# Layer 2's results turned to token rows by VectorE's 32x32 transposes instead of TensorE transposes, on one Trainium2 core

## The chip, the core and the metric

The kernel runs on one core of a Trainium2 chip. The metric is the device time of one execution in microseconds (us). TensorE (PE) multiplies, VectorE (DVE) and ScalarE (ACT) do the elementwise work, GpSimd (POOL) does almost nothing here, and SyncE (SP) issues every transfer, in program order.

## What is computed

```python
# q, k, v: (8 batches, 8 heads, 576 tokens, 64); x below is (4608 tokens, 512)
kv = einsum('bhsd,bhse->bhde', k, v)
out = einsum('bhsd,bhde->bhse', q, kv)                 # then rms-normalised per head
...
xn = x / rms * rms_g                                   # layer 1
x = (silu(xn @ w_gate) * (xn @ w_val)) @ w_out         # d_ff 1536
h = maximum(x @ w_in, 0.0)                             # layer 2
return h * h @ w_out2                                  # d_ff 2048, result (4608, 512)
```

## The kernel before

Activations are kept transposed: a block `j` holds 512 tokens as 4 tiles `c` of 128 features by 512 tokens. There are nine blocks. Every float32 product is done as three TensorE passes over a high and a low part of each operand (`split` makes the parts: ScalarE copies the high part at line 616, VectorE subtracts at line 617).

The work runs in stages of two blocks. Each stage has an x-stage (`x_stage`, the product with the first weight, line 711) and an h-stage (`h_stage`, the product with the second). Stages of layer 2 with two blocks use a seven-product scheme (Strassen-like), so their h-stage is `run_seven` (line 989): 28 steps of 12 matmuls, seven products `i` in the order 1, 2, 5, 6, 7, 3, 4, four steps each but for the first two, whose last steps come together. The stages of layer 2 are the blocks (0,1), (2,3), (4,5), (6,7) and, alone, (8). The lone block runs `run_last`, where activations are the stationary operand, so its result comes out as token rows by itself.

In an h-stage each step needs one operand tile `ho`, made from `raw` by `split`; the pool `hop` has three such tiles, so ScalarE starts tile k when TensorE has ended step k-3. For products 1, 2, 5 and 6 VectorE also updates `raw` with a subtraction (line 620). `h_result` takes a finished result: for product 2 (tiles 0 and 1 of the first block), product 7 (tiles 2 and 3 of the second) and product 3 (tiles 0 and 1 of the second) VectorE adds a saved copy (line 726); for product 4 (tiles 2 and 3 of the first block) ScalarE copies the PSUM bank (line 1042).

In layer 2 the result then lies as `c_t[j, c]`, features by tokens, and the output wants token rows. So during the next stage's x-stage `side_step` runs two kinds of step in turn, one every second tick (a tick comes after every six matmuls there): `out_tile` puts four TensorE transposes of 128x128 into a PSUM bank (line 1050), and `out_put` copies the bank with ScalarE (line 1058) and stores 128 rows of 2 KB (line 1061). That is four groups for a block, eight for a stage.

```python
    def tick():
        now[0] += 1
...
        for p, acc, step in (("side", "s", side_step), ("prep", "p", prep_step)):
```

Weights come as tiles `wt` of 512 KB, one for every 12 matmuls, in a ring of five (`W_RING`): the load of a tile is issued when TensorE has let go of the tile five before it. All loads and stores stand in SP's one queue. `after(n, fn)` issues something n ticks later. The last block's `out_halves` copies each finished PSUM bank in two halves, one on ScalarE, one on VectorE, and stores them.

Of the kernel before, what the change touches and what calls it, by code (L numbers as in the profile page):

```python
# [11 lines left out]
F32 = mybir.dt.float32  # L12
# [3 lines left out]
AF = mybir.ActivationFunctionType  # L16
# [27 lines left out]
def attn_moe_moe(  # L44
# [13 lines left out]
    nc = tc.nc  # L58
    B, S, DM = kv.shape[0], kv.shape[1], kv.shape[2] // 2
# [3 lines left out]
    KC = DM // 128  # L63
    T = 512
    NB = NT // T
    NQ = T // 128
# [10 lines left out]
    ps_att = ctx.enter_context(tc.tile_pool(name="ps_att", bufs=1, space=bass.MemoryType.PSUM))  # L77
# [8 lines left out]
    ident = const.tile([128, 128], F32, name="ident")  # L86
# [4 lines left out]
    x2d = [dram.tile([128, KC, T], F32, name=f"x2d{j}") for j in range(NB)]  # L91
# [4 lines left out]
    def new_tmp(name="t"):  # L96
        return tmp.tile([128, T], F32, tag="t", name=name)
# [182 lines left out]
    prep_q = deque()  # L280

    def prep_step(due=True):
        if prep_q and all(getattr(fn, "ready", lambda: True)() for fn in prep_q[0]):
            if not due and not all(getattr(fn, "landed", lambda: True)() for fn in prep_q[0]):
                return False
            for fn in prep_q.popleft():
                fn()
            return True
        return False
# [60 lines left out]
    def w_fetch():  # L350
        nxt = None if not streams[0] or len(w_have) == W_RING else next(w_todo, None)
        if nxt:
            pair, h, i = nxt
            while not all((key, h) in prepped for key in pair):
                assert prep_step(), nxt
            if isinstance(i, slice):
                wide.rotate(-1)
                t = xop.tile([128, 2, 2, 2, 256], F32R, tag=wide[0], name="ww")
                nc.sync.dma_start(out=t.bitcast(F32), in_=wd[pair][h][:, i])
                w_have.append((nxt, t))  # L360
                return
            t = wpool.tile([128, 2, 2, 256], F32R, tag="w", name="wt")
            nc.sync.dma_start(out=t.bitcast(F32), in_=wd[pair][h][:, i])
            w_have.append((nxt, [t[:, e] for e in range(2)]))
# [286 lines left out]
    def x_load(layer, blocks, b, q, rb):  # L651

        j, kh = blocks[int(b[1]) - 1], int(b[0]) - 1
        while layer == 1 and (j, 2 * kh + 1) not in x1_done:
            assert chain or due, j
            tick()
        t = raw_tile(q, rb, "xr")
        nc.sync.dma_start(out=t, in_=(x1d if layer == 1 else x2d)[j][:, 2 * kh:2 * kh + 2, :])
        return t
# [1 line left out]

    now = [0]
    due = {}
    side = deque()
    pace = {"side": 0.0, "prep": 0.0, "s": 0.0, "p": 0.0}

    def after(n, fn):
        due.setdefault(now[0] + n, []).append(fn)
# [4 lines left out]
        seq_n[0] += 1  # L673
        insort(chain, (t, seq_n[0], fn))

    def side_step():
        if side:
            for fn in side.popleft():
                fn()

    def tick():
        now[0] += 1
        for fn in due.pop(now[0], ()):
            fn()
        while chain and chain[0][0] <= now[0]:
            chain.pop(0)[2]()
        for p, acc, step in (("side", "s", side_step), ("prep", "p", prep_step)):
            pace[acc] += pace[p]
            while pace[acc] >= 1:
                if step is prep_step and prep_q and not prep_step(False):  # L690
                    pace[acc] = min(pace[acc], 2)
                    break
                pace[acc] -= 1
                if step is side_step:
                    step()

    def flush():
        while due:
            tick()
# [25 lines left out]
    def add(o, ps, t):  # L725
        nc.vector.tensor_tensor(out=o, in0=ps, in1=t, op=ALU.add)  # L726
# [8 lines left out]
    def x_stage(layer, blocks, early):  # L735
# [7 lines left out]
        for n, t in visits:  # L743
# [10 lines left out]
            if first[0] and (n, t) == (0, 2):  # L754
                while chain:
                    tick()
                t0 = now[0] + 1
                for j in range(stages[1][1][0], NB):
                    gap, period = (6, 47) if j < 5 else (8, 60)
                    if j == 2:  # L760
                        kv_events(j, t0, gap)
                        t0 += 28
                    o_events(j, t0, 5, t0 + (30 if j == 2 else 33), 4)
                    if j + 1 < B:
                        kv_events(j + 1, t0 + 17, gap)
                    t0 += period
# [69 lines left out]
                    tick()  # L836
            banks.extend([bk[2], bk[3], bk[0], bk[1]])

    c_t, late = {}, deque()

    def h_stage(layer, blocks, nxt):

# [188 lines left out]

    def h_result(layer, j, c, ps, t=None):

        if layer == 1:
            o = new_tmp("o")
        else:
            o = l2c.tile([128, T], F32, tag=f"c{c}_{j % 2}", name="c")
            c_t[j, c] = o
        if t is not None:
            add(o, ps, t)  # L1040
        else:
            nc.scalar.activation(out=o, in_=ps, func=AF.Copy)
        if layer == 1:
            after(5, lambda: nc.sync.dma_start(out=x2d[j][:, c, :], in_=o))

    def out_tile(j, i, pool=ps_att, tag=None):

        ps = pool.tile([128, DM], F32, tag=tag or "AB"[i % 2], name="ot")
        for c in range(KC):
            nc.tensor.transpose(  # L1050
                out=ps[:, c * 128:(c + 1) * 128], in_=c_t[j, c][:, i * 128:(i + 1) * 128], identity=ident
            )
        return ps

    def out_put(j, i, ps, eng, lag=2):
        t = new_tmp("ob")
        if eng is nc.scalar:
            nc.scalar.activation(out=t, in_=ps, func=AF.Copy)
        else:
            nc.vector.tensor_copy(out=t, in_=ps)  # L1060
        after(lag, lambda: nc.sync.dma_start(out=out[j * T + i * 128:j * T + (i + 1) * 128, :], in_=t))

    def out_halves(j, i, ps):
        rows = slice(j * T + i * 128, j * T + (i + 1) * 128)
        for eng, c in ((nc.scalar, slice(0, T // 2)), (nc.vector, slice(T // 2, T))):
            t = tmp.tile([128, T // 2], F32, tag="t", name="ob")
            if eng is nc.scalar:
                eng.activation(out=t, in_=ps[:, c], func=AF.Copy)
            else:
                eng.tensor_copy(out=t, in_=ps[:, c])  # L1070
            nc.sync.dma_start(out=out[rows, c], in_=t)

    def out_steps(blocks):
        st, got = [], {}
        for j in blocks:
            for i in range(NQ):
                st.append([lambda j=j, i=i: got.__setitem__((j, i), out_tile(j, i))])
                st.append([lambda j=j, i=i: out_put(j, i, got.pop((j, i)), nc.scalar)])
        return st


    with tc.manual_schedule():
        hops = [(hop, "hop")]
# [91 lines left out]
        for n, (layer, blocks) in enumerate(stages):  # L1175
            nxt = stages[n + 1] if n + 1 < len(stages) else None
            if layer == 2 and stages[n - 1][0] == 1:
                assert not chain
                l1.close()
                l2raw = l2.enter_context(tc.tile_pool(name="raw3", bufs=1))  # L1180
                l2c = l2.enter_context(tc.tile_pool(name="c", bufs=1))
            if 0 < n < len(preps):
                prep_q.extend(preps[n])
            in_hops[0] = n > 0
            pace["side"] = 0.5 if layer == 2 else 0
            pace["prep"] = 1.0 if n == 0 else len(prep_q) / (40 if n == 1 else 64)
            ahead, run = h_stage(layer, blocks, nxt)
            x_stage(layer, blocks, ahead)
            if n in h_preps:
                prep_q.extend(h_preps[n])  # L1190
                pace["prep"] = 1.0
            run()
            if n == 0:
                while prep_q:
                    assert prep_step()
                first[0], streams[0] = False, True
                in_use.clear()
                for _ in range(W_RING):
                    w_fetch()
            while side:  # L1200
                side_step()
            if layer == 2 and nxt:
                side.extend(out_steps(blocks))
        flush()
        l2.close()

# [44 lines left out]
```

## Time and profile before

| | |
|---|---|
| time, median of 3 runs | 1671.29 us (1670.45 to 1671.65) |
| time of the profiled execution | 1672.07 us |
| its span, first to last instruction | 1670.3 us |
| busy: TensorE, VectorE, ScalarE | 1649.6, 1011.8, 699.2 us |
| moved by DMA | 442.86 MB, mean 265 GB/s |

The profiled execution took 0.78 us more than the median, and 1.77 us of its time lie outside the span. Layer 2's first two-block stage hands its results to the x-stage that begins at 1107 us of the span.

### The profile page before, as it was taken

The page shows a single profiled execution, that of the slowest core. Times are in us where ns is not written, and L with a number is a line of the kernel's source. Part 1 is how long each engine was busy: PE and PEld are TensorE (multiplying, and loading weights), DVE is VectorE, ACT ScalarE, POOL GpSimd, SP SyncE. Part 2 cuts the span into 40 slices and gives each one's busy share as a digit, 9 for nine tenths or more (in the row PEclk, how much of TensorE's full clock was granted, in tenths as well). Part 3 has the DMA queues.
Part 4 walks back from the last instruction along what each step waited for, and adds up shares of the span by engine and source line. Part 5 has one row for each costly group of instructions (what it writes and reads, how often), then busy time and mean ns, then how long its engine had stood idle before and what let it go on. Part 6 is the DMA issues. An engine that isn't in the chain of part 4 may idle for free.

```text
span 1670.3 us, 21012 instructions
## 1 busy us (share of the span) xinstructions
PE 1649.6 (99%) x8048; PEld 1358.2 (81%) x8048; DVE 1011.8 (61%) x1351; ACT 699.2 (42%) x940; POOL 6.7 (0%) x19
## 2 busy tenths in 40 slices
PE   8899999999999999999999999999999999999999
PEld 7678878788888888788888888888888888888887
DVE  6755584656684658544774357864885587568431
ACT  4542553244554355443554323543453344334331
POOL 0100000000000000000000000000000000000000
PEclk9999999999999999999999999999999999999999
DMA  9885689998997899887998866767676767766682
GB/s 341 277 297 203 230 281 331 365 362 271 372 345 256 301 291 354 287 320 266 351 361 281 285 212 195 241 205 216 194 245 207 212 194 246 211 205 219 192 283 101
DMA packets 140898, 442.86 MB, mean 265 GB/s; under 512 B 13312, under 2 KB 14336, under 8 KB 135424
## 3 DMA queue, kind: packets, MB, share of 16 engines
q1 hardware_dynamic: 140800, 441.54, 77.6%
q8 instruction: 64, 1.05, 0.3%
q14 instruction: 34, 0.28, 0.0%
HBM read 343.97 MB, written 97.52 MB: 264 GB/s over the span
## 4 chain that ended last, share of the span: by engine, by line
PE 83%; DVE 2%; DMA 1%; ACT 1%; issue 1%; DVEq 0%
PE c L711 43%; PE acc L932 16%; PE a L989 10%; PE e L989 5%; PE last L959 3%; PE d L989 3%; DMA wt<-wd_g 1%; PE ops L443 1%; PE ot L1050 1%; PE kvps L403 1%; PE xps L538 1%; DVE ws L190 0%; ACT ws L187 0%; DVE ss L478 0%; DVE hr L781 0%
## 5 line engine op out<-in xcount | busy, mean ns | idle before, releaser
L711 PE MATMUL c<-xo,wt 128*128 128x512 f32 x3336 | 779.9, 392 | 3.5 <-DMA wt<-wd_g 2.7
L711 PEld LDWEIGHTS c<-xo,wt 128*128 128x128 f32 x3336 | 620.5, 188 | 133.8 <-DMA wt<-wd_g 4.6
L617 DVE TENSOR_TENSOR ho<-hr,ho 128x1024 fp32r<-128x1024 f32 x174 | 212.8, 1223 | 143.2 <-ACT ho L616 143.0
L616 ACT ACTIVATE ho<-hr 128x1024 fp32r<-128x1024 f32 x174 | 184.1, 1058 | 178.4 <-PE a L989 60.0
L932 PE MATMUL acc<-ho,wt 128*128 128x512 f32 x1008 | 232.5, 391 | 0.0
L932 PEld LDWEIGHTS acc<-ho,wt 128*128 128x128 f32 x1008 | 188.3, 188 | 39.4 <-issue 0.7
L722 ACT ACTIVATE s<-c 128x512 f32<-128x512 f32 x204 | 119.2, 595 | 142.4 <-PE c L711 140.2
L989 PE MATMUL a<-ho,wt 128*128 128x512 f32 x768 | 176.7, 389 | 0.0
L989 PEld LDWEIGHTS a<-ho,wt 128*128 128x128 f32 x768 | 144.2, 188 | 29.9
L726 DVE TENSOR_TENSOR c<-c,s 128x512 f32<-128x512 f32 x150 | 103.1, 687 | 101.6 <-PE c L711 95.5
L711 PE MATMUL c<-xo,ws 128*128 128x512 f32 x576 | 142.0, 401 | 3.4 <-ACT ws L187 2.8
L711 PEld LDWEIGHTS c<-xo,ws 128*128 128x128 f32 x576 | 107.6, 191 | 27.6 <-ACT ws L187 3.7
L617 DVE TENSOR_TENSOR xo<-xr,xo 128x1024 fp32r<-128x1024 f32 x53 | 64.7, 1222 | 98.0 <-ACT xo L616 97.9
L781 DVE TENSOR_TENSOR hr<-c,hr 128x512 f32<-128x512 f32 x108 | 73.8, 685 | 35.6 <-PE c L711 28.3
L989 PE MATMUL e<-ho,wt 128*128 128x512 f32 x384 | 88.3, 389 | 0.0
L776 ACT ACTIVATE r<-c 128x512 f32<-128x512 f32 x48 | 28.7, 598 | 136.6 <-PE c L711 136.6
L989 PEld LDWEIGHTS e<-ho,wt 128*128 128x128 f32 x384 | 72.1, 188 | 14.9
L620 DVE TENSOR_TENSOR hr<-hr 128x1024 f32<-128x1024 f32 x64 | 78.2, 1222 | 1.1
L777 DVE TENSOR_TENSOR hr<-c,r 128x512 f32<-128x512 f32 x48 | 33.2, 692 | 61.4 <-ACT r L776 61.3
L932 PE MATMUL acc<-ho,ws 128*128 128x512 f32 x288 | 68.9, 394 | 0.3 <-DVE ws L190 0.3
L616 ACT ACTIVATE xo<-xr 128x1024 fp32r<-128x1024 f32 x53 | 55.2, 1054 | 32.5 <-DVE xr L620 28.8
L190 DVE TENSOR_TENSOR ws<-wpl,ws 128x1024 fp32r<-128x1024 f32 x40 | 48.9, 1223 | 32.0 <-ACT ws L187 31.9
(85 smaller groups left out, 1234.7 us busy)
## 6 DMA issues: line engine op xcount, KB each, us to landing
wt<-wd_g SPq DMA_DIRECT2D x150, 512.0 KB, 6.5
wt<-wd_i SPq DMA_DIRECT2D x128, 512.0 KB, 4.2
wt<-wd_p SPq DMA_DIRECT2D x112, 512.0 KB, 4.7
wt<-wd_o SPq DMA_DIRECT2D x84, 512.0 KB, 5.0
wd_g<-ws SPq DMA_DIRECT2D x24, 1024.0 KB, 9.8
kvraw<-in_kv_dram SPq DMA_DIRECT2D x32, 512.0 KB, 7.2
wd_i<-ws SPq DMA_DIRECT2D x16, 1024.0 KB, 7.7
wd_p<-ws SPq DMA_DIRECT2D x16, 1024.0 KB, 8.6
```

The source lines that it names most:

```text
L190: nc.vector.tensor_tensor(out=st[h][:, :, 1, :], in0=quarters(st["sw"[1 - h]]), in1=st[h][:, :, 0, :].bitcast(F32), op=ALU.subtract,)
L616: nc.scalar.activation(out=dst[:, 0], in_=src, func=AF.Copy)
L617: eng.tensor_tensor(out=dst[:, 1], in0=src, in1=dst[:, 0].bitcast(F32), op=ALU.subtract)
L620: eng.tensor_tensor(out=o, in0=x, in1=y, op=ALU.subtract)
L711: nc.tensor.matmul(ps, lhsT=w[:, a, kc * 128:(kc + 1) * 128], rhs=x[:, b, kc, :], start=(start and n == 0 and kc == 0), stop=(n == 2 and k ...
L722: nc.scalar.activation(out=t, in_=ps, func=AF.Copy)
L726: nc.vector.tensor_tensor(out=o, in0=ps, in1=t, op=ALU.add)
L777: after(1, lambda: nc.vector.tensor_tensor(out=hr, in0=c, in1=t, op=ALU.mult))
L781: after(2, lambda: nc.vector.tensor_tensor(out=hr, in0=c, in1=hr, op=ALU.mult))
L932: nc.tensor.matmul(acc[c], lhsT=wt[:, a, (c % 2) * 128:(c % 2 + 1) * 128], rhs=x[:, b, e, :], start=(n == 0 and e == 0 and a + b == 0), st ...
L959: nc.tensor.matmul(acc[i].rearrange("p (r n) -> p r n", r=2), lhsT=x[:, b, e, i * 128:(i + 1) * 128], rhs=w[:, :, e, a, :], start=(n == 0 ...
L989: nc.tensor.matmul(ps, lhsT=w[e][:, a, d * 128:(d + 1) * 128], rhs=x[:, b, e, :], start=(i in (1, 2, 5) and q == 0 and e == 0 and a + b == 0),
```

## The change

The TensorE transposes of layer 2, the ScalarE copies behind them and `side_step` are gone. `rows_out` takes a result two ticks after it is done and lets VectorE transpose each of its 4 x 16 blocks of 32x32 (`nc.vector.transpose`, shown as STREAM_TRANSPOSE) into a tile `ob` of the block. Where an addition made the result, the addition now writes a temporary `o` and the transpose reads that; the results of product 4 are transposed straight out of PSUM, without ScalarE's copy.

A 32x32 transpose leaves each 32 x 32 piece in its own 32 partitions. So partition 32n + t of `ob` holds, for token 32b + t, the features of partitions 32n to 32n+31 of all four tiles. The host permutes the columns of the second weight (`swapaxes`) so that these 128 values are neighbours in the output: one run of 512 bytes. `rows_put` stores one quarter `n` of the partitions (32 partitions, 16 runs each, 256 KB), four times a block, two ticks apart, the first four ticks after the block's last transpose. In the last block the copies of `out_halves` read PSUM in runs of 32 to undo the permutation.

```diff
-        for p, acc, step in (("side", "s", side_step), ("prep", "p", prep_step)):
...
     def h_result(layer, j, c, ps, t=None):
 
-        if layer == 1:
-            o = new_tmp("o")
-        else:
-            o = l2c.tile([128, T], F32, tag=f"c{c}_{j % 2}", name="c")
-            c_t[j, c] = o
+        if layer == 2:
+            return rows_out(j, c, ps, t)
+        o = new_tmp("o")
...
-    def out_tile(j, i, pool=ps_att, tag=None):
-    def out_put(j, i, ps, eng, lag=2):
...
+    BL = 32
+    ob_t = {}
+
+    def rows_out(j, c, ps, t):
+
+        if j not in ob_t:
+            ob_t[j] = l2c.tile([128, T // BL, KC * BL], F32, tag=f"ob{j % 2}", name="ob"), set()
+        ob, have = ob_t[j]
+        o = ps
+        if t is not None:
+            o = new_tmp("o")
+            add(o, ps, t)
+
+        def turn():
+            nc.vector.transpose(
+                out=ob[:, :, c * BL:(c + 1) * BL], in_=o.rearrange("p (b t) -> p b t", t=BL)
             )
+            have.add(c)
+            if len(have) == KC:
+                for n in range(NQ):
+                    after(4 + 2 * n, lambda n=n: rows_put(j, n, ob))
+
+        after(2, turn)
+
+    def rows_put(j, n, ob):
+        part = slice(n * BL, (n + 1) * BL)
+        nc.sync.dma_start(
+            out=out[j * T:(j + 1) * T, n * 128:(n + 1) * 128].rearrange("(b t) x -> t b x", t=BL), in_=ob[part]
+        )
 
     def out_halves(j, i, ps):
         rows = slice(j * T + i * 128, j * T + (i + 1) * 128)
-        for eng, c in ((nc.scalar, slice(0, T // 2)), (nc.vector, slice(T // 2, T))):
+        got = ps.rearrange("p (c a f) -> p a c f", c=KC, f=BL)
+        for eng, n in ((nc.scalar, 0), (nc.vector, 1)):
             t = tmp.tile([128, T // 2], F32, tag="t", name="ob")
+            o = t.rearrange("p (a c f) -> p a c f", c=KC, f=BL)
...
-            if layer == 2 and nxt:
-                side.extend(out_steps(blocks))
...
-        "wo2": rows(moe2_w_out),
+        "wo2": rows(moe2_w_out.reshape(-1, 4, 4, 32).swapaxes(1, 2).reshape(-1, DM)),
```

The order on three engines moves as follows; the names are those of the code, and a row with x2 stands for two such instructions. On VectorE, in the h-stage of blocks (0,1), where product 2 is finished, the program had before

```order
L726 TENSOR_TENSOR c<-d,s 128x512 x2
L617 TENSOR_TENSOR ho<-hr,ho 128x1024
L620 TENSOR_TENSOR hr<-hr 128x1024
L617 TENSOR_TENSOR ho<-hr,ho 128x1024
L620 TENSOR_TENSOR hr<-hr 128x1024
```

and has now

```order
L717 TENSOR_TENSOR o<-d,s 128x512 x2
L1048 STREAM_TRANSPOSE ob<-o 128x16x32
L617 TENSOR_TENSOR ho<-hr,ho 128x1024
L620 TENSOR_TENSOR hr<-hr 128x1024
L1048 STREAM_TRANSPOSE ob<-o 128x16x32
L617 TENSOR_TENSOR ho<-hr,ho 128x1024
```

Two transposes now stand ahead of the operands of the steps that follow. On VectorE, from the end of product 3 into the next x-stage, there stood before

```order
L726 TENSOR_TENSOR c<-e,s 128x512 x2
L617 TENSOR_TENSOR ho<-hr,ho 128x1024 x2
L620 TENSOR_TENSOR xr<-xr 128x1024
L617 TENSOR_TENSOR xo<-xr,xo 128x1024
L726 TENSOR_TENSOR c<-c,s 128x512
```

and there stands now

```order
L717 TENSOR_TENSOR o<-e,s 128x512 x2
L1048 STREAM_TRANSPOSE ob<-o 128x16x32
L617 TENSOR_TENSOR ho<-hr,ho 128x1024
L1048 STREAM_TRANSPOSE ob<-o 128x16x32
L617 TENSOR_TENSOR ho<-hr,ho 128x1024
L1048 STREAM_TRANSPOSE ob<-a 128x16x32
L620 TENSOR_TENSOR xr<-xr 128x1024
L1048 STREAM_TRANSPOSE ob<-a 128x16x32
L617 TENSOR_TENSOR xo<-xr,xo 128x1024
L717 TENSOR_TENSOR c<-c,s 128x512
```

The transposes of `a` read PSUM, so they wait for TensorE's last matmuls of the stage, and the subtraction `xr` and the split `xo` for the next x-stage now stand behind that wait. On SP, at the change from the h-stage to the next x-stage, the stores stood one behind every second weight tile, the first as here behind eight tiles of the x-stage's weight:

```order
L363 DMA wt<-wd_i_0_141 128x1024
L363 DMA wt<-wd_i_0_143 128x1024
L1061 DMA out_dram<-ob 128x512
L363 DMA wt<-wd_i_0_143 128x1024
L363 DMA wt<-wd_i_1_144 128x1024
L1061 DMA out_dram<-ob 128x512
```

They now stand one behind every weight tile, eight in a row, the first of them five tiles earlier; these are the third to the sixth:

```order
L363 DMA wt<-wd_i_1_142 128x1024
L1060 DMA out_dram<-ob 32x16x128
L363 DMA wt<-wd_i_1_142 128x1024
L1060 DMA out_dram<-ob 32x16x128
L363 DMA wt<-wd_i_0_141 128x1024
L1060 DMA out_dram<-ob 32x16x128
L363 DMA wt<-wd_i_0_143 128x1024
L1060 DMA out_dram<-ob 32x16x128
```

So in eight consecutive steps each step carries one weight tile and one store. On TensorE nothing moves but that the 32 groups of four transposes are gone.

## Rows read from the trace of the kernel before

**Rows 1.** The page: busy us, share of the span and instructions of each engine.

```profile
PE 1649.6 (99%) x8048; PEld 1358.2 (81%) x8048; DVE 1011.8 (61%) x1351; ACT 699.2 (42%) x940; POOL 6.7 (0%) x19
```

**Rows 2.** Chain that ended last, 1090 to 1670: start us, us, what.

```profile
1107.26 2.72 PE c L711 x12
1109.98 0.44 PE ot L1050 x4
1110.42 5.49 PE c L711 x24
...
1151.90 35.41 PE c L711 x156
1187.31 8.16 PE a L989 x36
...
1209.07 10.88 PE e L989 x48
1219.95 21.76 PE a L989 x96
1241.71 10.88 PE e L989 x48
1252.59 10.88 PE a L989 x48
1263.47 2.72 PE c L711 x12
...
1575.89 2.72 PE c L711 x12
...
1623.31 43.53 PE last L959 x192
...
1667.28 0.42 DVE ob L1070
```

**Rows 3.** The tile ot: durations in ns, minimum/median/maximum, first and last start.

```profile
L1050 PE MATMUL ot<-ident,c x128: 270/272/273, 1109.8 to 1620.3; 128*128 128x128 f32 x128
L1058 ACT ACTIVATE ob<-ot x32: 587/593/599, 1112.4 to 1623.8; 128x512 f32<-128x512 f32 x32
```

**Rows 4.** VectorE's groups, shapes apart: busy us, mean ns | idle before.

```profile
L726 DVE TENSOR_TENSOR c<-d,s 128x512 f32<-128x512 f32 x8 | 5.1, 681 | 0.0
```

**Rows 5.** Timeline of VectorE, product 5: start us, us, instruction [idle before].

```profile
1210.37 1.28 DVE L726 TENSOR_TENSOR c<-d,s 128x512 f32<-128x512 f32 x2
...
1213.96 1.22 DVE L617 TENSOR_TENSOR ho<-hr,ho 128x1024 fp32r<-128x1024 f32 x1
```

**Rows 6.** Timeline of VectorE, product 3 and the next x-stage's start.

```profile
1247.12 1.22 DVE L617 TENSOR_TENSOR ho<-hr,ho 128x1024 fp32r<-128x1024 f32 x1
...
1257.58 1.22 DVE L620 TENSOR_TENSOR xr<-xr 128x1024 f32<-128x1024 f32 x1
1267.81 1.23 DVE L617 TENSOR_TENSOR xo<-xr,xo 128x1024 fp32r<-128x1024 f32 x1 [9.01 <-ACT xo L616]
```

**Rows 7.** Timeline of ScalarE at the same change of stage.

```profile
1262.15 0.60 ACT L1042 ACTIVATE c<-a 128x512 f32<-128x512 f32 x1 [5.74 <-PE a L989]
...
1266.72 2.00 ACT L616 ACTIVATE xo<-xr 128x1024 fp32r<-128x1024 f32 x2
```

**Rows 8.** Windows: engines busy us, granted clock, DMA share, GB/s.

```profile
1200.00:1222.00 22.00, 22.00 (x99) 18.23 (x98) 19.93 (x19) 10.68 (x12) 0.00 (x0) 1.00 0.58 195
...
1667.00:1670.30 3.30, 0.00 (x0) 0.00 (x0) 0.42 (x1) 0.25 (x1) 0.00 (x0) 1.00 0.41 135
```

**Rows 9.** DMA issues on the page and in the DMA view: KB each, us to landing.

```profile
wt<-wd_i SPq DMA_DIRECT2D x128, 512.0 KB, 4.2
...
out_dram<-ob SPq DMA_DIRECT2D x32, 256.0 KB, 4.7
```

**Rows 10.** Line 200 on SP: ns that issuing a 512-run store took.

```profile
L200 SPq DMA_DIRECT2D wd_p<-ws x16: 524/525/1204, 679.6 to 912.6; - x16
```

More of the change, by code (lines that the diff above doesn't have):

```diff
@@ L663, in attn_moe_moe @@
     due = {}
-    side = deque()
-    pace = {"side": 0.0, "prep": 0.0, "s": 0.0, "p": 0.0}
+    pace = {"prep": 0.0, "p": 0.0}
     def after(n, fn):
@@ L674, in at @@
         insort(chain, (t, seq_n[0], fn))
[L676 to L679, printed above, removed]
     def tick():
@@ L686, in tick @@
             chain.pop(0)[2]()
-        for p, acc, step in (("side", "s", side_step), ("prep", "p", prep_step)):
[L688 to L695, printed above, removed]
+        pace["p"] += pace["prep"]
+        while pace["p"] >= 1:
+            if prep_q and not prep_step(False):
+                pace["p"] = min(pace["p"], 2)
+                break
+            pace["p"] -= 1
     def flush():
@@ L837, in x_stage @@
             banks.extend([bk[2], bk[3], bk[0], bk[1]])
-    c_t, late = {}, deque()
+    late = deque()
     def h_stage(layer, blocks, nxt):
@@ L1042, in h_result @@
             nc.scalar.activation(out=o, in_=ps, func=AF.Copy)
-        if layer == 1:
-            after(5, lambda: nc.sync.dma_start(out=x2d[j][:, c, :], in_=o))
-    def out_tile(j, i, pool=ps_att, tag=None):
[L1048 to L1051, printed above, removed]
-            )
-        return ps
-    def out_put(j, i, ps, eng, lag=2):
[L1056 to L1061, printed above, removed]
+        after(5, lambda: nc.sync.dma_start(out=x2d[j][:, c, :], in_=o))
@@ L1066, in out_halves @@
             t = tmp.tile([128, T // 2], F32, tag="t", name="ob")
+            o = t.rearrange("p (a c f) -> p a c f", c=KC, f=BL)
             if eng is nc.scalar:
-                eng.activation(out=t, in_=ps[:, c], func=AF.Copy)
+                eng.activation(out=o, in_=got[:, 2 * n:2 * n + 2], func=AF.Copy)
             else:
[L1070 to L1079, printed above, removed]
+                eng.tensor_copy(out=o, in_=got[:, 2 * n:2 * n + 2])
@@ L1082, in attn_moe_moe @@
+            nc.sync.dma_start(out=out[rows, n * T // 2:(n + 1) * T // 2], in_=t)
     with tc.manual_schedule():
@@ L1184, in attn_moe_moe @@
             in_hops[0] = n > 0
-            pace["side"] = 0.5 if layer == 2 else 0
             pace["prep"] = 1.0 if n == 0 else len(prep_q) / (40 if n == 1 else 64)
@@ L1199, in attn_moe_moe @@
                     w_fetch()
-            while side:
-                side_step()
-            if layer == 2 and nxt:
-                side.extend(out_steps(blocks))
         flush()
```

## The prediction

> **What bounds the kernel.** I read the engines' busy shares first: TensorE is busy 99% of the span, VectorE 61%, ScalarE 42% [rows 1]. Then the chain that ended last, from 1090 us on: it is TensorE from end to end, one matmul group behind the other, until the last bank is copied out [rows 2]. So a microsecond that is taken from TensorE's queue in layer 2 comes off the time, as long as its operands, its weights and its PSUM banks still come early enough. The rest of the reading is about those three.
>
> In that chain the transposes of the results stand as pieces of 0.44 us among the x-stage's matmuls: a group of four, then 24 matmuls in 5.49 us, and so on [rows 2]. There are 32 groups, 128 transposes of 272 ns each that overlap in the array [rows 3].
>
> **The change, part by part.**
>
> *TensorE loses 32 groups.* The x-stage without them is priced by its own clean part: 156 matmuls in 35.41 us, 0.2270 us each [rows 2]. The x-stage that starts at 1107.26 ends at 1187.31, 80.05 us for 336 matmuls and eight groups. 336 x 0.2270 is 76.27 us, so eight groups cost 3.78 us. Three x-stages have this form. The fourth, from 1575.89 to 1623.31, has 192 matmuls: 47.42 - 43.58 = 3.84 us. The sum is 3 x 3.78 + 3.84 = 15.2 us. (The groups' own 0.44 us would make 14.1 us; the rest is what the matmuls next to them lose, and I take the difference of whole stages because it holds both.) The h-stage beside it checks the price: from 1187.31 to 1263.47, 76.16 us for 336 matmuls without any transpose [rows 2].
>
> *ScalarE loses 32 copies of 593 ns [rows 3] and the eight copies of product 4 [rows 7].* It is not in the chain; this is worth nothing.
>
> *VectorE gains 32 transposes of 128 x 512 values.* The trace has no such instruction. The nearest row is an addition of the same size and type, 681 ns [rows 4]; two of them one behind the other take 1.28 us, so each further one takes 0.60 us of the queue [rows 5]. From below I bound a transpose by that 0.60 us of queue time, from above by twice that, 1.2 us, for two passes over four-byte values. I take 0.60 us, as the addition has the same shape and type and reads two operands where the transpose reads one. [...]
>
> What covers them is the lead of the operands in the h-stage. A step is 12 matmuls, 76.16 / 28 = 2.72 us, and its low part is read in the third matmul, 0.45 us after its start. Two places are tight:
> - Product 5. Two transposes stand ahead of operand 11 (counted from 0). Its low part is done at 1213.96 + 1.22 = 1215.18 [rows 5]; step 11 begins 2.72 us before product 5's last step ends at 1219.95, at 1217.23 [rows 2], so it is read at 1217.68. Lead 2.50 us, against 2 x 0.60 = 1.2 us.
> - Product 3. Two transposes stand ahead of operand 23: done at 1248.34 [rows 6], step 23 begins 2.72 us before 1252.59 [rows 2], read at 1250.32. Lead 1.98 us, against 1.2 us. VectorE works there without a pause, so the whole 1.2 us arrives, and 0.8 us are left.
>
> So these cost nothing. The cover is gone at 0.99 us a transpose in product 3 and at 1.25 us in product 5. At 1.2 us each the first would cost 0.4 us a stage, 1.3 us in the three stages that have it in this form.
>
> *A new wait at the change of stage.* The transposes of product 4 wait for TensorE's last matmuls; behind them in VectorE's queue are the subtraction `xr` and the splits `xo` of the next x-stage. Before, ScalarE took the first of these banks at 1262.15 [rows 7], so the first transpose can start there too, then 1.2 us of `xr`, then the second transpose after 1263.5, done at about 1264.8. ScalarE takes up `xo` only at 1266.72 [rows 7] and VectorE waited 9.01 us for it until 1267.81 [rows 6]. The new wait lies in that idle time: nothing.
>
> *The stores.* Each is 256 KB as before, but 512 runs of 512 bytes from 32 partitions, and eight follow one another at one a step. For the price of a weight tile I take a stretch that moves hardly anything else: 195 GB/s at a DMA share of 0.58, that is 336 GB/s of capacity [rows 8], so 512 KB take 1.56 us of all engines. That leaves 2.72 - 1.56 = 1.16 us a step for a store. No row has 512-byte runs. The nearest is the tail, where only the last block's stores move, in runs of 1 KB: 135 GB/s at 0.41, or 329 GB/s [rows 8], so 0.80 us for a store. From below I take 0.80 us; from above, if a run costs the same whatever its length, 1.6 us. At 1.6 us the queue falls behind by 0.44 us a step, 3.5 us over eight. A weight tile is issued four steps, 10.9 us, before its use and lands in 4.2 us [rows 9]: 6.7 us to spare. I take nothing, as both ends are hidden; it holds up to 1.16 + 6.7 / 8 = 2.0 us a store. Issuing 512 runs costs SP 0.52 us [rows 10], well inside a step.
>
> [...]
>
> *The tail.* ScalarE's and VectorE's last two copies follow the last matmul as before [rows 2]; they read runs of 32 instead of one run. Between 0 and 0.4 us, the length of one such copy; I take 0.
>
> **Sum.** 1670.3 - 15.2 = 1655.1 us of span, 1656.9 us by the profiled execution's own time of 1672.07. That execution lies 0.78 us above the median, so for the median 1671.29 - 15.2 = **1656.1 us**.
>
> **Rivals.**
> 1. *The stores starve the weights; slower.* For: eight stores stand in eight steps, short runs, few partitions. Against: the tail's rate with half the run length lost nothing. The lag is 8 x (store - 1.16), less the 6.7 us to spare, four times. It eats the 15.2 us when a stage waits 3.8 us, that is at 2.47 us a store, a third of the tail's rate. At a quarter of it, 3.2 us, a stage waits 8 x 2.04 - 6.7 = 9.6 us, four stages 38 us: 1694 us.
> 2. *VectorE holds up the operands.* With queue time p for a transpose the stage waits (2p - 1.98) + (2p - 2.50). At p = 1.2 only the first counts: 1657.4 us. From p = 2.07 on the whole gain is gone. For: products 5 and 3 leave VectorE no pause. Against: it would take three to four times the time of an addition of the same size.
> 3. *Part of the gain is given back* by stores between 2.0 and 2.4 us or by both together: around 1663 us.
> 4. *The change doesn't do what it says*, TensorE's gaps staying for another reason: nothing in the chain has another end there; the 80.05 us against 76.16 us of the h-stage speak against it. No chance of its own.
>
> **How the numbers follow.** Forecast 0.80 (all hidden, 1655 to 1657.5 with the bounds of tail and transposes); rival 2 with 0.08, most of it under 1661; rival 3 with 0.05; rival 1 with 0.07. The range 1654.9 to 1661.0 us holds the forecast and the milder half of rivals 2 and 3, and leaves out about 0.14. Measurement tells about 0.2%, 3.3 us, from no change. Faster 0.91, within 0.2% 0.02, slower 0.07.
>
> **What would show it.** In the changed kernel's chain the x-stages of layer 2 should be one unbroken piece of 336 matmuls in 76.2 us, h-stages again 76.2 us. Transposes on VectorE should have a mean near 0.7 us. The weights' time to landing may rise by 1 to 4 us in the eight steps, with TensorE still unbroken. I am wrong if TensorE shows idle time before `wt` (rival 1) or before `ho` in products 5 or 3 (rival 2), or if a store takes more than 2.0 us of the DMA engines.

## The result and the profile after

The changed kernel takes 1654.24 us (median of 4 runs, 1653.4 to 1656.34) against 1671.27 us (4 runs) before: a ratio of 0.9901, interval 0.9884 to 0.9918. That is 17.0 us less, where 15.2 us were forecast, and 0.66 us below the low end of the range. The profiled execution took 1654.22 us, with a span of 1652.4 us.

The page's busy times of the changed kernel answer to [rows 1]:

```profile
PE 1632.0 (99%) x7920; PEld 1344.8 (81%) x7920; DVE 1029.6 (62%) x1383; ACT 678.5 (41%) x900; POOL 6.7 (0%) x19
```

TensorE still sets the end. The chain that ended last of the changed kernel (start us, us, what) answers to [rows 2]:

```profile
1104.99 76.16 PE c L702 x336
1181.15 8.16 PE a L980 x36
...
1257.31 76.16 PE c L702 x336
...
1409.63 76.16 PE c L702 x336
...
1561.95 43.52 PE c L702 x192
1605.47 43.53 PE last L950 x192
...
1649.44 0.42 DVE ob L1073
```

Each x-stage is one unbroken piece, 76.16 us where there were 80.05 and, in the last stage, 43.52 where there were 47.42. The h-stage between the first two pieces is 76.16 us, as before. From the first of these x-stages to the last bank's copy it is 544.45 us, against 1667.28 - 1107.26 = 560.02 before: 15.57 us less. But the first piece also starts 2.27 us earlier than before, at 1104.99 in place of 1107.26. **Those 2.27 us lie ahead of everything that the change touches.**

Their source is seen at the very start. Windows of the kernel before, then of the changed kernel, 10 to 20 us (PE busy, PEld, DVE, ACT, POOL, granted clock, DMA share, GB/s):

```profile
10.00:20.00 10.00, 8.35 (x84) 7.60 (x80) 4.49 (x7) 3.04 (x5) 0.00 (x0) 0.83 1.05 345
```

```profile
10.00:20.00 10.00, 7.36 (x92) 6.53 (x90) 6.18 (x10) 4.38 (x7) 0.00 (x0) 1.00 1.05 371
```

and TensorE's timeline of each:

```profile
11.33 0.69 PE L403 MATMUL kvps<-kvraw 128*64 128x64 f32 x16 [0.36 <-DMA kvraw<-in_kv_dram]
...
13.02 0.68 PE L403 MATMUL kvps<-kvraw 64*64 64x64 f32 x16 [0.36 <-DMA kvraw<-in_kv_dram]
14.63 5.46 PE L443 MATMUL ops<-kvb,qt 128*128 128x128 f32 x32 [0.93 <-ACT kvb L415]
...
32.90 3.08 PE L711 MATMUL c<-xo,ws 128*128 128x512 f32 x12
```

```profile
14.45 3.84 PE L443 MATMUL ops<-kvb,qt 128*128 128x128 f32 x32 [0.93 <-ACT kvb L415]
...
31.20 3.08 PE L702 MATMUL c<-xo,ws 128*128 128x512 f32 x12
```

TensorE's matmuls stand in the same order in both programs, there and up to the x-stage at 1105 us. In the profiled execution of before, TensorE waited twice for a load of kv (0.36 us each) and then, as in the changed kernel, 0.93 us for the copies of kv. The 32 matmuls behind that ran for a while at a granted clock of 0.50 (15 to 18 us; 1.00 there in the changed kernel): 5.46 us in place of 3.84. So the first weight product began at 32.90 in place of 31.20, 1.70 us of the 2.27.

What the change brought, in the tile `ob` of the changed kernel (ns, minimum/median/maximum):

```profile
L1048 DVE STREAM_TRANSPOSE ob<-o x24: 697/702/705, 1053.1 to 1553.6; 128x512 f32<-128x512 f32 x24
L1048 DVE STREAM_TRANSPOSE ob<-a x8: 706/717/718, 1103.7 to 1562.0; 128x512 f32<-128x512 f32 x8
```

A transpose costs what the addition of [rows 4] costs and 21 to 36 ns more. VectorE's timeline at products 5 and 3 and at the change of stage, of the changed kernel, answers to [rows 5, 6]:

```profile
1208.39 0.70 DVE L1048 STREAM_TRANSPOSE ob<-o 128x512 f32<-128x512 f32 x1
1209.02 1.18 DVE L617 TENSOR_TENSOR ho<-hr,ho 128x1024 fp32r<-128x1024 f32 x1
...
1242.03 1.22 DVE L617 TENSOR_TENSOR ho<-hr,ho 128x1024 fp32r<-128x1024 f32 x1
...
1255.99 0.72 DVE L1048 STREAM_TRANSPOSE ob<-a 128x512 f32<-128x512 f32 x1 [4.48 <-PE a L980]
1256.63 1.18 DVE L620 TENSOR_TENSOR xr<-xr 128x1024 f32<-128x1024 f32 x1
1257.73 0.71 DVE L1048 STREAM_TRANSPOSE ob<-a 128x512 f32<-128x512 f32 x1
1261.65 1.23 DVE L617 TENSOR_TENSOR xo<-xr,xo 128x1024 fp32r<-128x1024 f32 x1 [3.21 <-ACT xo L616]
```

The transpose holds the queue from 1208.39 to 1209.02. Operand 23 (1242.03) is done at 1243.25, read at 1181.15 + 23 x 2.72 + 0.45 = 1244.16: 0.9 us are left. The two transposes out of PSUM wait for TensorE in time in which VectorE had nothing else, and `xo` still waits 3.21 us for ScalarE.

In the eight steps of the stores the DMA engines' busy share is 1.00. A window of that stretch of the changed kernel, and the DMA view of it, answer to [rows 8, 9]:

```profile
1254.61:1276.31 21.70, 21.70 (x97) 17.97 (x97) 15.52 (x20) 6.81 (x10) 0.00 (x0) 1.00 1.00 286
```

```profile
wt<-wd_i SPq DMA_DIRECT2D x8, 512.0 KB, 4.7
out_dram<-ob SPq DMA_DIRECT2D x7, 256.0 KB, 5.1
```

A share of 1.00, yet the weights land in 4.7 us (4.2 before) and TensorE is busy for all 21.70 us. The 286 GB/s are what the steps ask for: a weight tile and a store, 0.786 MB in 2.72 us, are 289 GB/s.

### The profile page after: what moved, and what is told of

It is laid out like the page before. It is cut to its first block, busy times and chain, and to the rows that moved or that the text cites. A ratio compares the mean times of both kernels' runs of the same rounds, so it can differ in the third digit from the quotient of the medians.

```text
span 1652.4 us, 20718 instructions
## 1 busy us (share of the span) xinstructions
PE 1632.0 (99%) x7920; PEld 1344.8 (81%) x7920; DVE 1029.6 (62%) x1383; ACT 678.5 (41%) x900; POOL 6.7 (0%) x19
## 4 chain that ended last, share of the span: by engine, by line
PE 83%; DVE 2%; DMA 1%; ACT 1%; issue 1%; DVEq 0%
PE c L702 43%; PE acc L923 17%; PE a L980 11%; PE e L980 5%; PE last L950 3%; PE d L980 3%; DMA wt<-wd_g 1%; PE ops L443 1%; PE kvps L403 1%; PE xps L538 1%; DVE ws L190 0%; ACT ws L187 0%; DVE ss L478 0%; DVE hr L772 0%; DVE y L460 0%
## 5 line engine op out<-in xcount | busy, mean ns | idle before, releaser
L702 PE MATMUL c<-xo,wt 128*128 128x512 f32 x3336 | 770.2, 391 | 3.7 <-DMA wt<-wd_g 3.0
L717 DVE TENSOR_TENSOR hr<-c,s 128x512 f32<-128x512 f32 x54 | 37.2, 688 | 51.0 <-PE c L702 50.6
```

The costliest lines, as they stand in the source:

```text
L702: nc.tensor.matmul(ps, lhsT=w[:, a, kc * 128:(kc + 1) * 128], rhs=x[:, b, kc, :], start=(start and n == 0 and kc == 0), stop=(n == 2 and k ...
```

## The experiments

Two things had to be told apart: whether the 15.57 us are TensorE's slots alone, and whether the rest is the change's or a throw of layer 1. "The stretch of layer 2" is the time from the start of its second x-stage to the start of the last bank's copy. The first four runs are about the start.

**after_again**: the changed kernel unchanged.

> The changed kernel once more, unchanged. Its layer 2 (from the first x-stage that held transposes to the last bank's copy) took 544.45 us against 560.02 us before, 15.57 us less; 1.8 us more were lost or won in the first 200 us, where both programs issue the same instructions. Theory (a throw of the start: when a load of kv lands late, TensorE waits, its granted clock falls to the lower level, and 1 to 2 us are lost): layer 2 again 15.57 us shorter to within 0.1 us, start differing from profile to profile; times spread from 1653 to 1656.5, median 1654 to 1656. Rival (the change itself quickens the start): the first TensorE stage always without a fall of the clock, all times at or below 1654.5.

1654.62 us (4 runs, 1654.22 to 1655.05), 0.9904 (0.9888 to 0.9919) of the kernel before, whose median was now 1670.44 us over 15 runs from 1668.9 to 1672.97. Stretch 1649.84 - 1105.38 = 544.46 us. The distance is 15.8 us, not 17.0. Every time fits the theory's band, and three of four lie above the rival's 1654.5.

**before_again**: the kernel before unchanged.

> The kernel before once more, for a second profile of its start. Theory (a throw): the granted clock between 10 and 20 us may be 1.00 this time, and then layer 1's end stands 1.5 to 2 us earlier; from the first x-stage with transposes to the end again 560.0 us. Rival (the change quickens the start): again a clock of about 0.83 between 10 and 20 us, and layer 1's end at 1107 us.

The chain of this second profile of the kernel before:

```profile
1109.40 2.72 PE c L711 x12
...
1669.42 0.42 DVE ob L1070
```

The stretch is 560.02 us again. The granted clock between 10 and 20 us was 1.00 this time, against the rival. But the expected early end of layer 1 did not come: 1109.40 is the latest of all, 1674.21 us. The chain shows where, at 825 us, deep in layer 1:

```profile
824.82 0.32 SPq L363
...
825.19 12.15 DMA wd_p<-ws
...
837.42 1.07 ACT ws L187
```

A store of prepared weights took 12.15 us to land, ScalarE's next preparation waited for it, and TensorE's matmuls waited up to 1.87 us behind that. Up to 822 us this execution of the kernel before is level with the profile of the changed kernel (one and the same matmul starts at 821.90 and at 821.95); from 860 us on it is 4.4 us behind. So layer 1 has more than one place where a microsecond or two is lost: here the waits behind one transfer's landing (1.24 and 1.87 us), at the start the 1.62 us by which the 32 matmuls at the lower granted clock took longer (5.46 in place of 3.84).

**after_fill, before_fill**: six idle matmuls in the 0.93 us wait behind the first kv products, in each kernel.

```diff
             kv_mm(0, c, psum, "b5")
-            keep(2 if c < 4 else 0)
+            keep(2 if c < 4 else 6)
```

> The changed kernel with six idle matmuls in the 0.93 us in which TensorE waits for the first kv copies (the kept matmuls behind the last of the first five kv loads, 6 in place of 0). Theory (a throw of the start): with that wait filled the clock stays at its upper level through the first q products, so the slow starts go and the median is 0 to 1.5 us lower than that of the changed kernel, spread below 1.5 us. Rival: no difference, since the start is fixed by the program.

> The kernel before with the same six idle matmuls. Theory (a throw of the start that the kernel before mostly loses): 1669 to 1670.5 us, 1 to 2 us under the kernel before, and the distance to the changed kernel with the same fill is the 15.6 us of layer 2. Rival (something in the program, not the clock): 1671.3 us as before, and the distance stays at 17 us.

1654.72 us (4 runs, 1653.89 to 1657.09) and 1671.23 us (11 runs, 1670.03 to 1673.32; ratio to the kernel before 1.0004, 0.9996 to 1.0013). The clock between 10 and 20 us was 1.00 in the profile with the fill, as it was without it in before_again and after_again. The expected gain of 1 to 2 us failed: the start's clock is not what the median hangs on. The spread of the four runs, 3.2 us, is not below the expected 1.5 either, and the distance between the two kernels is 16.5 us, between the theory's 15.6 and the rival's 17. The stretches were 544.45 us (after_fill) and 560.02 us (before_fill).

**dead_transposes**: 32 groups of TensorE transposes put back without use (in the last stage three of the eight fall behind the x-stage, into the lone block's second product); the stretch holds all 32.

```diff
+    def dead(n, ob):
+        ps = ps_att.tile([128, DM], F32, tag="AB"[n % 2], name="ot")
+        for c in range(KC):
+            nc.tensor.transpose(out=ps[:, c * 128:(c + 1) * 128], in_=ob[:, 4 * n + c, :], identity=ident)
```

> The changed kernel with 32 groups of four TensorE transposes put back into the x-stages as dead weight: they read the finished tile ob and write a PSUM bank that nobody reads. The stretch from layer 2's second x-stage to the last bank's copy took 544.45 us in each of three profiles of the changed kernel, 560.02 us in two of the kernel before. Theory (the gain is TensorE's slots and nothing else): 560.0 us again, to within 0.3 us, so all of it comes back, without ScalarE's copies and with the new stores. Rival (part of the gain is ScalarE's or the store order's): between 545 and 558 us.

The chain of this kernel:

```profile
1105.28 6.80 PE c L702 x30
1112.52 5.49 PE c L702 x24
...
1185.34 8.16 PE a L980 x36
...
1665.31 0.42 DVE ob L1079
```

Stretch 560.03 us, an x-stage of 80.06 us: all 15.57 us came back (15.58), and the time is that of the kernel before, 1670.85 us (ratio 1.0003, 0.9994 to 1.0013). Its layer 1 is the changed kernel's, so this also bounds what the change can do to layer 1: nothing beyond that interval, about -1 to +2 us.

This profile also had the start's fall of the clock, with the changed kernel's layer 1. A window of it and TensorE's timeline:

```profile
10.00:20.00 10.00, 8.23 (x80) 7.46 (x74) 4.68 (x8) 3.22 (x6) 0.00 (x0) 0.83 1.04 355
```

```profile
14.39 5.47 PE L443 MATMUL ops<-kvb,qt 128*128 128x128 f32 x32 [0.93 <-ACT kvb L415]
...
32.73 3.08 PE L702 MATMUL c<-xo,ws 128*128 128x512 f32 x12
```

So the fall does not belong to the kernel before, which answers the rival of after_again. Nor does it decide when layer 1 ends: the first weight product begins 1.53 us later than in the changed kernel (32.73 and 31.20), layer 2's second x-stage 0.29 us later (1105.28 and 1104.99). In between TensorE waits for weights, in the changed kernel 1.39 us for `wd_g`, up to 330.56.

**stores_twice**: every quarter stored twice, the second time into scratch.

```diff
-        nc.sync.dma_start(
-            out=out[j * T:(j + 1) * T, n * 128:(n + 1) * 128].rearrange("(b t) x -> t b x", t=BL), in_=ob[part]
-        )
+        for to in (out[j * T:(j + 1) * T], twin[j % 2]):
+            nc.sync.dma_start(out=to[:, n * 128:(n + 1) * 128].rearrange("(b t) x -> t b x", t=BL), in_=ob[part])
```

> The changed kernel with each store of a quarter made twice, the second copy into a scratch tensor. In the eight steps the DMA engines were already busy with a share of 1.00. Theory (a store takes about 1.16 us of all engines, weights have 6.7 us to spare): the queue falls behind by 1.16 us a step, 9.3 us over eight, so the stretch of layer 2 grows by about 2.6 us for each of four stages, 10 us, to some 555 us. Rival (the engines had room left, 0.8 us a store): a lag of 3.5 us, hidden, 544.5 us. Rival (a store costs 1.6 us): lag 16 us, four times 9.6 us, some 583 us.

1654.85 us, stretch 1650.08 - 1104.26 = 545.82 us: 1.4 us more, not 10 and not 0. TensorE's chain breaks for weights once in the last x-stage; a second place gives 0.26 us (an x-stage of 76.42):

```profile
1561.49 13.61 PE c L703 x60
...
1578.40 6.96 DMA wt<-wd_i
1585.41 20.69 PE c L703 x90
```

In the eight steps the engines moved 299 GB/s, and the weights landed in 6.8 us. A step asks for 1 MB, 1.049 MB / 0.299 = 3.5 us of work in 2.72: a lag of 0.8 us a step, 6.3 us over eight, about the 6.7 us to spare. With the prediction's 1.56 us for the weight tile, a store of this shape thus cost about 1.0 us by estimate, not the 1.16 that the full share suggested.

**rows_2k_128, rows_512_128, rows_2k_32**: the same bytes as runs of 2 KB from 128 partitions, 512 bytes from 128, 2 KB from 32; the edits in that order.

```diff
     def rows_put(j, n, ob):
+        nc.sync.dma_start(out=out[j * T + n * 128:j * T + (n + 1) * 128, :], in_=ob[:, 4 * n:4 * n + 4].rearrange("p b x -> p (b x)"))
...
+        nc.sync.dma_start(
+            out=out[j * T:(j + 1) * T, n * 128:(n + 1) * 128].rearrange("(b t) x -> t b x", t=128), in_=ob[:, 4 * n:4 * n + 4]
+        )
...
+        nc.sync.dma_start(
+            out=out[j * T + n * 128:j * T + (n + 1) * 128, :].rearrange("(b t) x -> t b x", t=BL),
+            in_=ob[part].rearrange("p (b a) x -> p b (a x)", a=4),
+        )
```

> The changed kernel with stores of the same bytes at the same places in the queue, but as 128 partitions with runs of 2 KB (the values land in the wrong rows, so this is for its time only). Theory (short runs from few partitions cost DMA time that is hidden): the stretch of layer 2 stays at 544.45 us, the DMA share in the eight steps falls from 1.00 to about 0.85 to 0.9 and the weights' time to landing from 4.9 to about 4.5 us. Rival (runs and partitions cost nothing): share and landing as in the changed kernel.

> The changed kernel with stores in runs of 512 bytes, but from all 128 partitions, four runs each (values in the wrong rows: for its time only). The share of the DMA engines in the eight steps was 1.00 with 512-byte runs from 32 partitions and 0.94 with 2 KB runs from 128. Theory A (the length of a run costs it): 0.99 to 1.00. Theory B (the few partitions cost it): 0.94. Layer 2's stretch 544.45 us in either case.

> The changed kernel with stores in runs of 2 KB from 32 partitions, four runs each (values in the wrong rows: for its time only). Theory A (the length of a run costs it): share 0.94. Theory B (the few partitions cost it): 0.99 to 1.00. Layer 2's stretch 544.45 us in either case.

The times were 1654.61, 1655.30 and 1654.80 us (one run each). The stretch was 544.45 us in the first, 544.46 and 544.45 in the others. The window of the eight steps at the second of the x-stages, of the three kernels in that order:

```profile
1255.00:1276.70 21.70, 21.70 (x97) 17.96 (x97) 15.52 (x20) 6.80 (x10) 0.00 (x0) 1.00 0.95 294
```

```profile
1255.65:1277.35 21.70, 21.70 (x97) 17.96 (x97) 15.52 (x20) 6.81 (x10) 0.00 (x0) 1.00 1.00 294
```

```profile
1255.20:1276.90 21.70, 21.70 (x97) 17.96 (x97) 15.52 (x20) 6.81 (x10) 0.00 (x0) 1.00 0.95 294
```

The length of the run made the difference (0.95 at 2 KB, 1.00 at 512 bytes); the number of partitions made none (0.95 from 128 and from 32 with 2 KB, 1.00 from 128 and, in the changed kernel, from 32 with 512 bytes). The difference is smaller than I expected (0.85 to 0.9), and the weights' landing, 4.9 us in the first against 4.7 in the changed kernel, did not improve.

**rows_2k_128_twice**: the 2 KB shape, stored twice.

```diff
+        for to in (out[j * T:(j + 1) * T], twin[j % 2]):
+            nc.sync.dma_start(out=to[n * 128:(n + 1) * 128, :], in_=ob[:, 4 * n:4 * n + 4].rearrange("p b x -> p (b x)"))
```

> The changed kernel with each store made twice, as 2 KB runs from 128 partitions (values in the wrong rows: for its time only). With 512-byte runs from 32 partitions, twice, TensorE waited 1.4 us for weights in all and the weights landed in 6.8 us. Theory (the shape of the stores costs about 0.06 of the share, 0.16 us a store): two stores a step save 0.3 us, 2.6 us over eight steps, so TensorE never waits (544.45 us) and weights land in under 6.5 us. Rival (bytes alone count): 545.8 us and 6.8 us as with the short runs.

1654.12 us (one run), stretch 544.45 us, the weights land in 5.2 us. A window of the eight steps of this kernel, and of stores_twice:

```profile
1254.50:1276.20 21.70, 21.70 (x97) 17.96 (x97) 15.52 (x20) 6.81 (x10) 0.00 (x0) 1.00 1.01 371
```

```profile
1253.89:1275.59 21.70, 21.70 (x97) 17.96 (x97) 15.51 (x20) 6.81 (x10) 0.00 (x0) 1.00 1.02 299
```

At shares of 1.01 and 1.02 the long runs moved 371 GB/s and the short ones 299. So the price of the short runs is real, 1.049 / 0.299 - 1.049 / 0.371 = 0.68 us for two stores, 0.34 us each, or more: the steps ask for 1.049 MB in 2.72 us, 386 GB/s, so the long runs were close to what was asked and need not have been at their limit. The changed kernel, which stores once, hides it: its stretch is 544.45 us, and that of rows_2k_128 too.

**turns_twice**: each transpose given twice.

```diff
+            for _ in range(2):
                 nc.vector.transpose(
```

> The changed kernel with each 32x32 transpose instruction given twice on VectorE (the second writes the same values). A transpose took 0.70 us, 0.62 us of the queue. Theory (the leads of 2.50 us in product 5 and 1.98 us in product 3 are what covers them): four in a row of operands make 2.48 us, so product 3 waits 0.5 us in three stages and product 5 not at all: the stretch of layer 2 grows by 1.5 us to 546.0. Rival (the cover is larger, for VectorE catches up where ScalarE is late): 544.5 us. Rival (smaller): 550 us or more.

1660.58 us, stretch 1655.79 - 1107.92 = 547.87 us: 3.4 us more, twice the expected 1.5 (and 1.45 us more in the first h-stage, ahead of the stretch). TensorE's timeline of this kernel shows both places, each in the third matmul of its step,

```profile
1205.67 8.78 PE L980 MATMUL e<-ho,wt 128*128 128x512 f32 x38
1214.68 2.57 PE L980 MATMUL e<-ho,wt 128*128 128x512 f32 x10 [0.23 <-DVE ho L617]
1217.08 21.92 PE L980 MATMUL a<-ho,wt 128*128 128x512 f32 x96
1238.84 8.77 PE L980 MATMUL e<-ho,wt 128*128 128x512 f32 x38
1248.24 2.57 PE L980 MATMUL e<-ho,wt 128*128 128x512 f32 x10 [0.63 <-DVE ho L617]
1250.65 1.52 PE L980 MATMUL a<-ho,wt 128*128 128x512 f32 x6
```

and VectorE's timeline the ends of the two operands:

```profile
1213.44 1.18 DVE L617 TENSOR_TENSOR ho<-hr,ho 128x1024 fp32r<-128x1024 f32 x1
...
1246.97 1.21 DVE L617 TENSOR_TENSOR ho<-hr,ho 128x1024 fp32r<-128x1024 f32 x1
```

38 matmuls are three steps and two: operands 11 and 23, the ones named. Product 5 takes 11.41 us from 1205.67 to the next product at 1217.08 in place of 10.88, a loss of 0.53; product 3 takes 11.81, a loss of 0.93. The h-stages of blocks (2,3) and (4,5) lose both, that of (6,7) only the 0.52 us of product 5: 2 x 1.45 + 0.52 = 3.42 us. The expectation had counted three waits of product 3 into the stretch, of which the first stands ahead of it.

It left out three things. Two equal transposes took 1.44 us (1208.34), more than twice the 0.70 of one, so a pair held the queue for 1.37 us, to 1209.71, and not 1.24. TensorE took up the operand 0.06 us after its end (1214.62 and 1214.68, 1248.18 and 1248.24). And the ten matmuls behind the stop took 2.40 and 2.41 us to the next product, where ten in a stream take 2.27 (12 in 2.72). By the leads of 2.50 and 1.98 us that makes 0.24 + 0.19 = 0.43 us for product 5 and 0.76 + 0.20 = 0.96 us for product 3, against 0.53 and 0.93.

## Why the prediction was right and where it was wrong

**The mechanism held in every part.** TensorE's slots were the whole gain of layer 2 (dead_transposes gave back 15.57 of 15.57 us). VectorE's transposes cost 0.62 us of queue where 0.60 was taken, and nothing on the path (the two passes behind the upper bound of 1.2 us were an assumption of mine, which no run shows); turns_twice shows the two tight places where they were named. The new wait at the change of stage lay in idle time. The stores were hidden: an estimated 1.0 us each, between the bounds of 0.80 and 1.6. No tail cost: 2.96 us from the start of the last copy to the end of the span, 3.02 before. None of the rivals came. The weights' time to landing rose by 0.5 us, less than the 1 to 4 us that were held possible. One price was read too simply: a rate divided by its DMA share gave 336 GB/s for the engines, and rows_2k_128_twice moved 371 GB/s, so the 1.56 us for a weight tile, and with it the 1.0 us for a store, are rough; the sum does not hang on them. The few partitions that rival 1 counts in its favour cost nothing that the runs show: stores from 32 partitions had the same share as from 128 (0.95 with 2 KB runs, 1.00 with 512 bytes), at 286 to 294 GB/s with the weights beside them.

**Two steps failed, by size.** The first is "156 matmuls in 35.41 us, 0.2270 us each" as the price of a clean x-stage. That piece still held a few hundredths from the last transpose group next to it; a clean x-stage is 76.16 us, not 76.27. The h-stage beside it, named there as the check, had the right figure: with it the sum is 3 x 3.89 + 3.90 = 15.57 us, what was measured to a hundredth. That is 0.4 us; with it the forecast is 1655.7 us, still 1.5 us above the measured 1654.24.

The second, which put the result outside the range, is the step "for the median 1671.29 - 15.2" and the low end of 1654.9 us under it. Every term with bounds was already taken at its best one and none gives the low end, so its 1.2 us below the forecast had to hold the throw of both medians, and the prediction prices none. It took the median of before as known, as three runs lay within 1.2 us. More runs of the same kernel range over 4 us (1668.9 to 1672.97 in one session), with a median of 1670.44. In the profiles, layer 2's second x-stage starts between 1106.12 and 1109.40 with the program of before (before_fill included) and between 1104.26 and 1106.03 with those of the change whose first h-stage has no added wait, dead_transposes among them. From that start to the end of the execution it is 564.8 us with the program of before and 549.2 us with the changed one, in every such profile but stores_twice and dead_transposes, which change layer 2 itself. So all of the spread arises ahead of it, and 15.57 us of the 17.0 are the change's. The other 1.46 us are throws of both medians, as far as the repeats show: the median of before fell by 0.83 us from the four runs to the fifteen (1671.27 to 1670.44), that of the changed kernel rose by 0.38 (1654.24 to 1654.62), and the distance became 15.8 us, which leaves 0.25. That the first distance came out as large as 17.0 us was for the most part luck.

Whether a few tenths of layer 1 belong to the change stays open. For it: all three distances, 17.0, 15.8 and with the fill 16.5 us, lie above 15.57, and the three profiles with the program of before have the three latest starts. Against it: TensorE's matmuls stand in the same order up to there, before_again was level with the changed kernel up to 822 us, and dead_transposes, with the changed kernel's layer 1, has the time of the kernel before to 0.1 us (interval about -1 to +2).

**The theory formed after the result fell in part.** That the start's clock makes the spread was seen in one pair of profiles (1.70 us), but filling the wait changed no median, the slowest profile had no fall there (it lost its time from 825 us on), and dead_transposes had the fall and made most of it good before layer 1's end. What is shown is several throws in layer 1, not one.

## What to carry to other kernels

When one engine is the whole chain, price an edit by the difference of whole stages, and take the clean price from a stage that has none of the removed work, not from what is left of the same stage. Before a range narrower than the kernel's own spread is given, look for stretches ahead of the change that vary from run to run, as here behind a store that took 12.15 us to land: the kernel before reached layer 2's second x-stage at 1107.26 us in one profile and at 1109.40 in another, which is no part of the effect; compare the changed stretch by itself. Work that is put on a half-idle engine is paid by the lead of what stands behind it, place by place (here 2.50 and 1.98 us; with each transpose given twice, 0.53 and 0.93 us were lost there), and a share of 1.00 on the DMA engines was no stall by itself: TensorE was busy for all 21.70 us of that window.

## What the runs showed of the hardware that was not expected

- The DMA share did not grow in proportion to the bytes moved. With 2 KB runs it was 0.95 at 294 GB/s and 1.01 at 371 GB/s, when each store was made twice; with 512-byte runs 1.00 at 286 GB/s, all that was asked, and 1.02 at 299 GB/s, where TensorE had to wait for weights.
- Stores in runs of 512 bytes cost, by an estimate from the two kernels that store twice, at least 0.34 us more for 256 KB than in runs of 2 KB (299 and 371 GB/s, half of the bytes weight loads); from 32 or from 128 partitions made no difference to the share (0.95 with 2 KB, 1.00 with 512 bytes).
- A float32 transpose of 128 x 512 in 32x32 blocks took VectorE 702 ns out of SBUF and 717 ns out of PSUM, hardly more than the 681 ns of an addition of that size.
- Four float32 TensorE transposes of 128x128 cost 0.49 us of TensorE's time among matmuls (15.57 us / 32), though each is shown with 272 ns.
